# Attention and Hyena gate on one core: inverse transform of two batches on 193 columns and their mirror, with a new instruction sequence

## The chip, the cores and the metric

The kernel runs on one core of a Trainium2 chip. A core has a matrix engine, TensorE (PE in the profile, its weight loads apart as PEld), and three engines for element work: VectorE (DVE), ScalarE (ACT) and GpSimd (POOL). SyncE (SP) only issues DMAs. Each engine works off its own queue of instructions in order and waits on semaphores for the others. Operands lie in SBUF, a memory of 128 partitions; TensorE writes its results to PSUM, of which the kernel uses four slots of two banks. The metric is the device time of one execution in microseconds (us); less is better.

## The reference

Inputs are q, k, v with 4 batches, 8 heads, 768 positions and 64 numbers per head, and the matrices of the gate. Heads are either "retrieval" (full causal attention) or "streaming" (4 sink positions and a window of 64).

```python
scores = np.where(mask, scale * q @ k.transpose(0, 1, 3, 2), -1e9)     # per head
a = np.exp(scores - scores.max(-1)); a = a / (a.sum(-1) + 1e-09)
x = (a @ v).transpose(0, 2, 1, 3).reshape(B, S, H * D)                 # B=4, S=768, H*D=512
...
proj = x @ w_proj
x1, x2, x3 = proj[..., :D], proj[..., D:2*D], proj[..., 2*D:]          # D = 512 here
X2 = np.fft.rfft(x2, n=S, axis=1)
H = np.fft.rfft(filter_fft, n=S, axis=0)[None, :, :]
x2_conv = np.fft.irfft(X2 * H, n=S, axis=1)
y = x1 * x2_conv * x3
return (y @ w_out).astype(np.float32)
```

## The kernel before

**Two halves.** Attention is done in 16 units n = 0 to 15 of two heads each; units 4b to 4b+3 belong to batch b. The gate follows batch by batch, so that the gate of batch b runs while the attention of batch b+1 does. After unit 15 only the gate of batches 2 and 3 is left.

**An order written out by hand.** The whole fast path is one straight-line program. A string named FAST lists its steps; a word such as `oe3.1/s` or `c3.0.0@2` names a step, after "/" the engine that does it (v VectorE, s ScalarE, p GpSimd) and after "@" the PSUM slot that it takes. Steps without "/" have a fixed engine. A loop at the end of the function calls the steps in the order of the string, so the string sets the order of every engine's queue, and semaphores only what data and buffers ask for. Of SBUF the buffers are fixed too: a step that writes one waits for its last readers.

**Attention steps.** `lq`, `lk`, `lv` load (L908, L927, on the SP queue), `cq`, `ck` and from unit 8 on `cqk` cast q and k to bf16, with the source in one of three rotating buffers, two of which are named qk_ahead. `T` transposes the result: for units 0 to 7 on TensorE (L952), from unit 8 on as a DMA transposition on the SP queue (L962). `sc` are the scores (L990), `ex` the exponential (L1007), `mk` masks, `at` the product with v (L1050; v carries a column of ones, f_v_aug and its copy f_v_x), `rec` and `nm` the division (L1056, L1067). `fd`, `fe`, `fA`, `fS`, `fb`, `fr` add and subtract mirrored positions of a unit's output (f_fo, f_uv, f_br), which shortens the forward transform; `W` does that transform on TensorE (L1103 to L1111) and `We` evicts it to f_xh. `tn` brings the attention output into transposed form, for later units as a DMA transposition (L1132).

**Gate steps of batch b.** `X` (L1154) multiplies f_xh by w_proj, which gives the spectrum of x2 in three tiles t of 128 frequencies, real and imaginary part beside each other; `Xe` evicts them to bf16. `sw` swaps the halves of tile 2 by two DMAs (L1179, f_Xw). `pa`, `pb`, `pc` multiply by the filter's spectrum HAB and add: P, the product of spectra (all through the helper line L544). `x1` and `x3` are the other two projections (L1189), `xs` the eviction of x1. `c` (L1227) is the inverse transform of a block cb of 128 channels: r = 0 gives the part of the result that is even about the middle, r = 1 the odd part, each over 384 positions, from three matmuls with 384 columns each (cosine and sine tables Gi as the moving operand):

```python
for m, (t, u, tile_no) in enumerate(INVERSE[r]):
    nc.tensor.matmul(ps[:, r, 0:HS], lhsT=P(b)[:, t, u, ch], rhs=Gi()[:, tile_no],
                     start=(m == 0), stop=(m == 2))
```

Here HS = 384 and S = 768. `ce` copies the even part to SBUF (L541, f_evs, which lies in the buffer angle), `cv` (L1238) adds and subtracts the odd part, still in PSUM, and writes the 768 positions of the convolution in bf16 to f_conv, which lies in the buffer turns. There are two such buffers, for even and odd cb. `g` (L1208, L1212, L1214) multiplies x1 or the convolution by x3, `y` (L544) the convolution by what is left, into f_gy; `gh` (L1219) is the last half row of block 3 of batch 3. `o` (L1262; L1257 in halves for the row tile i = 5 of batch 3) multiplies by w_out, `oe` evicts to f_o and `st` stores.

**The end.** `rest` issues eight blank matmuls (L586). Steps `gd0` to `gd4` (L655 to L674) check that the row sums are sane: `gd0`, `gd1`, `gd2` reduce on VectorE, `gd3` is a one-column matmul, `gd4` writes a flag named `other`. `late` (L579) is a small cast that reads the last evictions. Then all engines read `other` (L1314) and skip a general path if it is 0.

## Time and profile before

| what | us |
|---|---|
| median of three runs (lowest, highest) | 183.8 (183.39, 184.66) |
| span of the profiled execution (the profile gives no other time of it) | 182.1 |
| TensorE busy in it | 172.8 |
| VectorE busy in it | 149.8 |
| ScalarE busy in it | 145.3 |
| GpSimd busy in it | 77.5 |

A page of the profile groups the instructions of one execution by line, engine and shape. "f_P<-f_X,f_HAB 128x1024 bf16" means that P was written from X and HAB, 1024 elements in each of 128 partitions. "x4 | 8.9, 2215" is the count, the busy time in us and the mean duration of one in ns; what follows is the idle time of the engine just before, with what ended it. A timeline row has the start, the duration and the same words; idle time stands in brackets at its end. In the chain of waits each row is a stretch of the path that ended last. L544 and L541 are lines of helpers that many steps share, so their rows are told apart by the names of the operands. Busy times of instructions that overlap on one engine are counted once, so a row "x2" may be shorter than twice one.

### The profile page before, as it was taken

The numbers are of one execution on the slowest core, as the hardware profiler recorded it, in microseconds if no ns is written. First come the engines' busy times: TensorE is split into PE (matmuls) and PEld (weight loads), VectorE is DVE, ScalarE is ACT, GpSimd is POOL, SyncE is SP. The second block draws the span as 40 slices with busy tenths as digits, with TensorE's granted clock in tenths as the row PEclk, the third lists the DMA queues.
The fourth block names the chain that finished last, engine by engine and source line by source line (L and its number), as shares of the span: only waits on it lengthen the run. The fifth ranks groups of instructions, "written<-read, shape, count | busy, mean of one in ns | idle before, by whom it ended". The sixth has DMA issues, their size and how long they took to land.

```text
span 182.1 us, 4374 instructions
## 1 busy us (share of the span) xinstructions
PE 172.8 (95%) x1684; PEld 103.6 (57%) x1700; DVE 149.8 (82%) x298; ACT 145.3 (80%) x196; POOL 77.5 (43%) x94
## 2 busy tenths in 40 slices
...
GB/s 159 356 203 287 294 257 200 204 290 230 232 224 166 184 228 198 116 214 142 265 217 200 150 231 166 123 208 243 228 153 112 184 0 0 58 2 119 127 277 184
DMA packets 78396, 33.83 MB, mean 186 GB/s; under 512 B 67618, under 2 KB 74786, under 8 KB 78370
## 3 DMA queue, kind: packets, MB, share of 16 engines
...
q8 instruction: 14, 0.23, 0.6%
...
q14 instruction: 12, 0.10, 0.2%
...
## 4 chain that ended last, share of the span: by engine, by line
PE 82%; DVE 8%; ACT 4%; DMA 3%; issue 1%
PE f_x_ps L1189 23%; PE f_X_ps L1154 12%; PE f_out_ps L1262 10%; PE f_c_ps L1227 9%; PE f_sc L990 8%; PE f_att L1050 7%; DMA f_qkT<-f_qk_bf 3%; PE f_qkT_ps L952 2%; PE f_sc L1001 2%; PE warm L454 2%; PE f_xt_ps L1123 2%; ACT f_pT L1007 1%; DVE f_HAB L691 1%; PE f_W_ps L1103 1%; PE f_W_ps L1105 1%
## 5 line engine op out<-in xcount | busy, mean ns | idle before, releaser
L1007 ACT ACTIVATE f_pT<-f_sc 128x1024 bf16<-128x1024 f32 (+3 forms) x68 | 58.5, 914 | 3.6 <-PE f_sc L990 2.0
L1189 PE MATMUL f_x_ps<-f_xT,f_wproj 128*128 128x384 bf16 x256 | 46.9, 326 | 0.0
L1189 PEld LDWEIGHTS <-f_wproj 128*128 128x128 bf16 x256 | 23.9, 98 | 17.4 <-issue 1.6
L990 PE MATMUL f_sc<-f_qkT 64*128 64x128 bf16 (+3 forms) x328 | 20.9, 242 | 2.4 <-DMA f_qkT<-f_qk_bf 1.4
L1154 PE MATMUL f_X_ps<-f_wproj,f_xh 128*128 128x512 bf16 x90 | 22.1, 379 | 0.6 <-issue 0.2
L544 POOL TENSOR_TENSOR f_fo<-f_attn 128x384 bf16<-128x384 bf16 x15 | 14.6, 990 | 18.4 <-DVE f_attn L1067 17.3
L1262 PE MATMUL f_out_ps<-f_wout,f_gy 128*128 128x512 bf16 x86 | 22.0, 379 | 0.3
L990 PEld LDWEIGHTS <-f_qkT 64*128 64x128 bf16 x328 | 11.4, 94 | 13.0 <-issue 7.9
L1238 DVE TENSOR_TENSOR turns<-angle,f_c_ps 128x384 bf16<-128x384 f32 x32 | 16.3, 550 | 2.6 <-ACT angle L541 1.3
L1227 PE MATMUL f_c_ps<-f_Gi,f_P 128*128 128x384 bf16 x96 | 18.2, 326 | 0.1
L1050 PEld LDWEIGHTS <-f_pT 128*128 128x128 bf16 x472 | 16.2, 97 | 2.4 <-issue 0.4
L1050 PE MATMUL f_att<-f_v_aug,f_pT 128*128 128x65 bf16 x392 | 17.0, 193 | 0.0
L541 ACT COPY f_o<-f_out_ps 128x1024 f32<-128x1024 f32 (+2 forms) x15 | 12.1, 818 | 6.2 <-PE f_out_ps L1262 5.1
L541 ACT CAST f_X<-f_X_ps 128x1024 bf16<-128x1024 f32 x12 | 12.1, 1016 | 4.9 <-PE f_X_ps L1154 4.9
L1067 DVE TENSOR_TENSOR f_attn<-f_att,f_recs 128x768 bf16<-128x768 f32 x16 | 15.1, 951 | 0.6
L544 POOL TENSOR_TENSOR f_P<-f_X,f_HAB 128x1024 bf16<-128x1024 bf16 x4 | 8.9, 2215 | 14.5 <-ACT f_X L541 14.5
L544 POOL TENSOR_TENSOR f_gy<-turns,f_gy 128x768 bf16<-128x768 bf16 x5 | 8.5, 1710 | 14.6 <-DVE turns L1238 14.6
L1154 PEld LDWEIGHTS <-f_xh 128*128 128x128 bf16 x96 | 8.9, 97 | 10.2 <-issue 0.5
L1262 PEld LDWEIGHTS <-f_gy 128*128 128x128 bf16 x92 | 8.5, 98 | 8.8 <-POOL f_uv L544 0.4
L541 ACT COPY angle<-f_c_ps 128x384 f32<-128x384 f32 x15 | 7.2, 478 | 7.7 <-PE f_c_ps L1227 5.4
L1227 PEld LDWEIGHTS <-f_P 128*128 128x128 bf16 x96 | 9.1, 98 | 6.0 <-issue 0.2
L537 POOL CAST f_qk_bf<-qk_ahead 128x768 bf16<-128x768 f32 (+1 forms) x9 | 8.0, 900 | 8.7 <-DMA qk_ahead<-in_k_dram 3.4
...
## 6 DMA issues: line engine op xcount, KB each, us to landing
...
```

Source lines behind the costliest of these rows:

```text
L537: nc.gpsimd.tensor_copy(out=out, in_=in_)
L541: nc.scalar.copy(out=out, in_=in_)
L544: (nc.gpsimd if now["engine"] == "p" else nc.vector).tensor_tensor(out, a, b, op)
L990: nc.tensor.matmul(sc[:, bank, col:col + 128 * cnt], lhsT=keys, rhs=qkT(n)[rows, 0, 128 * i:128 * (i + cnt)], start=(col == 0 or not biase ...
L1007: nc.scalar.activation(out=pT(n)[:, c, :, 0:w], in_=held[f"sc.{n}.{c}"][:, :, 0:w], func=AF.Exp, scale=SCALE)
L1050: nc.tensor.matmul(att[:, hh, 65 * i:65 * i + 65], lhsT=pT(n)[:, c, bank, col:col + 128], rhs=values, start=(z == 0), stop=(z == len(here) ...
L1067: nc.vector.tensor_mul(attn(n).rearrange("p i hh d -> p hh i d"), rows[:, :, :, 0:64], recs()[:, n][:, :, :, None].to_broadcast([128, 2, N ...
L1154: nc.tensor.matmul(ps[:, u, :], lhsT=xh(b)[:, cc, chain, 128 * part:128 * part + 128], rhs=wproj()[:, cc, DM:2 * DM], start=(cc == 0), sto ...
L1189: nc.tensor.matmul(ps[:, s, 0:HS], lhsT=wproj()[:, cc, part * DM + cb * 128:part * DM + (cb + 1) * 128], rhs=xT(b)[:, cc, s * HS:s * HS + HS],
L1227: nc.tensor.matmul(ps[:, r, 0:HS], lhsT=P(b)[:, t, u, ch], rhs=Gi()[:, tile_no], start=(m == 0), stop=(m == 2))
L1238: fn(conv[:, half * HS:half * HS + HS], held[f"evs.{b}.{cb}"], held[f"c_ps.{b}.{cb}"][:, 1, 0:HS])
L1262: nc.tensor.matmul(ps[:, i % 2, :], lhsT=gy(b)[:, cb, i * 128:(i + 1) * 128], rhs=wout()[:, cb, :], start=(cb == 0), stop=(cb == NC - 1))
```

## The change

**Fewer columns.** The even and the odd part are each made of two waves, one of which is symmetric and the other antisymmetric about position 192. For batches 2 and 3 (MIRROR) the inverse computes each wave at 193 positions alone, and the rest by mirroring. Per channel block and r there is one matmul of 386 columns (the tile that both waves share, against a new table Gb that holds it for both halves) and two of 193 columns, where there were three of 384. `ce` now copies 386 columns, `cv` has 386 columns and writes fp32 to `parts`, which lies with the copied even part in a qk_ahead buffer that attention no longer needs. Two new steps `cw` on VectorE for each block add and subtract the two halves and write the convolution in bf16, the second of them with the positions reversed. There are 16 of them.

**Smaller parts.** The new steps Gz, Gb0, Gb1, Gn fill the table Gb (one memset on GpSimd, two copies on ScalarE, a copy and a memset of one partition on VectorE). H0.0 and H1.0 write HAB once, 512 wide, where they wrote it twice, and `pa` for t = 0 and 1 reads it by broadcast.

**A new sequence.** FAST is replaced as a whole: 32 instructions go from GpSimd to VectorE, 28 from VectorE to GpSimd, 21 from ScalarE to VectorE, 23 the other way, 10 from ScalarE to GpSimd and 4 back. Among the moves are the casts cqk9, cqk10 and cqk13, from ScalarE to GpSimd. Steps gd1 to gd4 stand at the very end.

```diff
+MIRROR = (2, 3)
...
-cv3.3.0 x33.3.0 y3.2/v st2.5 st2.3 gd3@3 o3.0.0@2 o3.4.0@1 y3.3/v g3.3 gh o3.0.1 gd4 oe3.0/s o3.4.1 o3.1.0@0 o3.1.1
...
+cw3.3.1/v x33.3.1 y3.2/v o3.4.0@2 st2.5 o3.0.0@3 oe2.3/s o3.1.0@0 cw3.3.0/v y3.3/v g3.3 gh o3.4.1 oe3.4/s o3.0.1
...
+    Gb = C("Gb", [128, 2, 2, 194], BF16)
...
+    wave = lambda part, rows, tiles: Gi()[rows, tiles].rearrange("p t m f -> p t (m f)")[:, :, 0:193]
...
+            ev(Gb()[rows, :, half, 0:193], wave(half, rows, slice(2, 6, 3)))
...
+        nc.vector.tensor_copy(out=Gb()[64:65, 1, 0, 0:193], in_=wave(0, slice(64, 65), slice(5, 6))[:, 0])
+        nc.vector.memset(Gb()[64:65, 1, 1], 0.0)
...
-        scaled(f"H{t}.0", lambda t=t: HAB()[:, t, 0:2, :],
-               lambda t=t: FP(t)[:, 0, None, :].to_broadcast([128, 2, DM]), 2.0 / S)
+        scaled(f"H{t}.0", lambda t=t: HAB()[:, t, 0, :], lambda t=t: FP(t)[:, 0], 2.0 / S)
...
-                two(P(b)[:, t], held[f"X.{b}.{t}"], HAB()[:, t, 0:2], ALU.mult)
+                real = HAB()[:, t, 0:2] if t == 2 else HAB()[:, t, 0, None].to_broadcast([128, 2, DM])
+                two(P(b)[:, t], held[f"X.{b}.{t}"], real, ALU.mult)
...
+                    if b in MIRROR:
+                        (t0, u0, a), (t1, u1, z), (t2, u2, shared_tile) = INVERSE[r]
+                        waves = lambda tile_no: Gi()[:, tile_no].rearrange("p m f -> p (m f)")[:, 0:193]
+                        both = ps[:, r, 0:386].rearrange("p (h n) -> p h n", h=2)
+                        nc.tensor.matmul(both, lhsT=P(b)[:, t2, u2, ch], rhs=Gb()[:, shared_tile // 3, :, 0:193],
+                                         start=True, stop=False, skip_group_check=True)
+                        nc.tensor.matmul(both[:, 0], lhsT=P(b)[:, t0, u0, ch], rhs=waves(a), start=False, stop=True,
+                                         skip_group_check=True)
+                        nc.tensor.matmul(both[:, 1], lhsT=P(b)[:, t1, u1, ch], rhs=waves(z), start=False, stop=True,
+                                         skip_group_check=True)
+                        return
...
+            if b in MIRROR:
+                space = first[cb % 2].rearrange("p a h t d -> p (a h t d)")
+                parts = space[:, 0:772].rearrange("p (z n) -> p z n", z=2)
+                even = space[:, 772:1158]
...
+                    ev(even[:, 0:386], held[f"c_ps.{b}.{cb}"][:, 0, 0:386])
...
+                        fn(parts[:, half, 0:386], even[:, 0:386], held[f"c_ps.{b}.{cb}"][:, 1, 0:386])
...
+                        if half == 0:
+                            two(conv[:, :, 0:192], parts[:, :, 0:192], parts[:, :, 193:385], ALU.add)
+                        else:
+                            two(conv[:, :, 192:384], parts[:, ::-1, 192:0:-1], parts[:, ::-1, 385:193:-1], ALU.subtract)
```

**What stands where: the cast of unit 12.** In the rows below the first word is the line (the helper L541 of before is L543 now), then the operation, and output and inputs with the program's numbers. This is ScalarE's queue before, between the last exponentials of unit 11 and the gate of batch 1; `f_qk_bf_12` is the cast, `f_X_1_0` an eviction Xe1.0, `angle` the step xs1.2, `f_v_x2` a copy of v:

```order
L1007 ACTIVATE f_pT_10_1590<-f_sc_10_2_1727 128x1024
L541 CAST f_X_1_0_1765<-f_X_ps_1_0_1712 128x1024
L1007 ACTIVATE f_pT_11_1703<-f_sc_11_2_1735 128x1024
L541 CAST angle_87<-f_x1_ps_1_2_1754 128x768
L541 COPY f_v_x2_270<-f_v_aug2_248 64x520
L541 CAST f_qk_bf_12_1848<-qk_ahead0_66 128x1536
L541 COPY f_xT_2_1645<-f_xt_ps_9_1784 128x768
```

And now:

```order
L1026 ACTIVATE f_pT_10_1576<-f_sc_10_2_1732 128x1024
L1026 ACTIVATE f_pT_11_1718<-f_sc_11_2_1739 128x1024
L543 CAST f_qk_bf_12_1772<-qk_ahead0_66 128x1536
L543 CAST f_X_1_0_1778<-f_X_ps_1_0_1727 128x1024
L543 CAST angle_87<-f_x1_ps_1_2_1783 128x768
L543 COPY f_v_x2_133<-f_v_aug2_249 64x520
L543 COPY f_o_0_2_1855<-f_out_ps_0_2_1749 128x1024
L543 COPY f_xT_2_1645<-f_xt_ps_9_1819 128x768
```

The cast has moved ahead of Xe1.0, xs1.2 and the copy of v.

The same place on the SP queue, which issues the loads and DMA transpositions, before (`f_Xw` are the swaps of batch 1, `f_qkT` the transposition of unit 12, `f_xT` one of tn):

```order
L908 DMA qk_ahead_66<-in_q_dram 128x6x64 x2
L1179 DMA f_Xw_1719<-f_X_2_1671 64x1024
L927 DMA f_v_f_13_1721<-in_v_dram 128x6x64 x2
L1179 DMA f_Xw_1719<-f_X_2_1671 64x1024
L908 DMA f_qk_f_14_1762<-in_q_dram 128x6x64 x2
L908 DMA qk_ahead_69<-in_q_dram 128x6x64 x2
L962 DMA_TRANSPOSE f_qkT_1885<-f_qk_bf_1848 128x12x128
L1132 DMA_TRANSPOSE f_xT_1645<-f_attn_1905 128x6x128
```

And now:

```order
L927 DMA qk_ahead_66<-in_k_dram 128x6x64 x2
L946 DMA f_v_f_13_1769<-in_v_dram 128x6x64 x2
L1357 DMA out_dram<-f_o_0_1431 128x2x512
L1199 DMA f_Xw_1794<-f_X_2_1704 64x1024
L927 DMA qk_ahead_69<-in_q_dram 128x6x64 x2
L1199 DMA f_Xw_1794<-f_X_2_1704 64x1024
L981 DMA_TRANSPOSE f_qkT_1891<-f_qk_bf_1772 128x12x128
L927 DMA f_qk_f_14_1896<-in_q_dram 128x6x64 x2
L1151 DMA_TRANSPOSE f_xT_1645<-f_attn_1914 128x6x128
```

The load of unit 14 (f_qk_f_14) has moved behind the transposition, the second swap from ahead of both loads to a place behind the one that is left, and a store stands ahead of the first swap.

**What stands where: the products of batch 3.** VectorE's queue before, from the last cv of batch 2 to the middle of the products (`f_m` is what pb writes, `f_P` what pa and pc write, `f_sane` the step gd0):

```order
L1238 TENSOR_TENSOR turns<-angle,f_c_ps_2_2547 128x384
L1095 SCALAR_TENSOR_TENSOR f_br_2616<-f_uv_2585,f_fo_2558 128x256
L1238 TENSOR_TENSOR turns<-angle,f_c_ps_2_2547 128x384
L535 CAST f_xh_2470<-f_W_ps_2639 128x768
L544 TENSOR_TENSOR turns<-turns,f_x1s_3_2321 128x768
L1208 TENSOR_TENSOR f_gy_2676<-angle,f_x_ps_0_2647 128x768
L1212 TENSOR_TENSOR f_gy_2036<-turns,f_x_ps_3_2590 128x768
L544 TENSOR_TENSOR f_P_2702<-f_X_1_2690,f_HAB 128x1024
L544 TENSOR_TENSOR f_m_3_2_2734<-f_Xw_2687,f_HAB 128x1024
L655 TENSOR_SCALAR f_sane<-f_recs 128x192
L544 TENSOR_TENSOR f_P_2702<-f_P_2702,f_m_3_2_2734 128x1024
L544 TENSOR_TENSOR f_P_2702<-f_X_0_2704,f_HAB 128x1024
```

And now (`turns<-qk_ahead` is cw, `qk_ahead<-qk_ahead,f_c_ps` is cv):

```order
L546 TENSOR_TENSOR turns<-qk_ahead_69 128x2x192 x2
L1273 TENSOR_TENSOR qk_ahead_66<-qk_ahead_66,f_c_ps_2_2598 128x386
L1228 TENSOR_TENSOR f_gy_2665<-angle,f_x_ps_0_2655 128x768
L1273 TENSOR_TENSOR qk_ahead_66<-qk_ahead_66,f_c_ps_2_2598 128x386
L1232 TENSOR_TENSOR f_gy_2074<-turns,f_x_ps_3_2612 128x768
L546 TENSOR_TENSOR turns<-qk_ahead_66 128x2x192
L546 TENSOR_TENSOR f_P_2697<-f_X_2_2680,f_HAB 128x1024
L546 TENSOR_TENSOR turns<-qk_ahead_66 128x2x192
L546 TENSOR_TENSOR f_m_3_1_2726<-f_X_1_2695,f_HAB 128x1024
L546 TENSOR_TENSOR f_P_2697<-f_X_1_2695,f_HAB 128x1024
L546 TENSOR_TENSOR f_m_3_2_2744<-f_Xw_2689,f_HAB 128x1024
L546 TENSOR_TENSOR f_P_2697<-f_P_2697,f_m_3_1_2726 128x1024
```

The cw of batch 2 now stand among cv and the first product, and more of the products are on this engine. GpSimd's queue at that place before:

```order
L544 TENSOR_TENSOR f_gy_2036<-turns,f_gy_2036 128x768
L544 TENSOR_TENSOR f_P_2702<-f_X_2_2668,f_HAB 128x1024
L544 TENSOR_TENSOR f_m_3_1_2728<-f_X_1_2690,f_HAB 128x1024
L544 TENSOR_TENSOR f_P_2702<-f_P_2702,f_m_3_0_2742 128x1024
L544 TENSOR_TENSOR f_gy_2676<-turns,f_gy_2676 128x768 x2
```

And now:

```order
L546 TENSOR_TENSOR f_uv_2580<-f_fo_2517 128x2x128
L546 TENSOR_TENSOR f_uv_2580<-f_fo_2517 128x256
L546 TENSOR_TENSOR f_br_2596<-f_fo_2517,f_uv_2580 128x256
L546 TENSOR_TENSOR turns<-turns,f_x1s_3_2339 128x768
L546 TENSOR_TENSOR f_gy_2074<-turns,f_gy_2074 128x768 x2
L546 TENSOR_TENSOR f_gy_2665<-turns,f_gy_2665 128x768
```

Before these were y2.2, three products of batch 3, then y3.0 and y3.1. Now, behind the folds of unit 14, they are y2.3, y2.0, y2.2 and y3.1: the products and y3.0 have gone to VectorE, y2.3 and y2.0 have come from it.

**What stands where: the last blocks.** VectorE's queue before, from the inverse of batch 3 to its end (L665 is gd2, L674 gd4):

```order
L1238 TENSOR_TENSOR turns<-angle,f_c_ps_0_2758 128x384 x2
L665 TENSOR_REDUCE f_right<-f_sane 128x1
L1238 TENSOR_TENSOR turns<-angle,f_c_ps_1_2767 128x384 x2
L1238 TENSOR_TENSOR turns<-angle,f_c_ps_2_2783 128x384 x2
L1238 TENSOR_TENSOR turns<-angle,f_c_ps_3_2798 128x384 x2
L544 TENSOR_TENSOR f_gy_2676<-turns,f_gy_2676 128x768
L544 TENSOR_TENSOR turns<-turns,f_x1s_3_2755 128x768
L1214 TENSOR_TENSOR f_gy_2676<-turns,f_x_ps_3_2832 128x384
L1219 TENSOR_TENSOR f_gy_2676<-turns,f_x_ps_3_2832 128x384
L674 TENSOR_SCALAR other<-f_rows_right,differ 1x1
```

And now:

```order
L1273 TENSOR_TENSOR qk_ahead_69<-qk_ahead_69,f_c_ps_1_2765 128x386 x2
L1273 TENSOR_TENSOR qk_ahead_66<-qk_ahead_66,f_c_ps_0_2771 128x386 x2
L546 TENSOR_TENSOR turns<-qk_ahead_66 128x2x192 x2
L546 TENSOR_TENSOR turns<-qk_ahead_69 128x2x192 x2
L546 TENSOR_TENSOR f_gy_2665<-turns,f_gy_2665 128x768
L1273 TENSOR_TENSOR qk_ahead_66<-qk_ahead_66,f_c_ps_2_2803 128x386 x2
L1273 TENSOR_TENSOR qk_ahead_69<-qk_ahead_69,f_c_ps_3_2821 128x386 x2
L546 TENSOR_TENSOR turns<-qk_ahead_66 128x2x192 x2
L546 TENSOR_TENSOR turns<-qk_ahead_69 128x2x192
L546 TENSOR_TENSOR f_gy_2665<-turns,f_gy_2665 128x768
L546 TENSOR_TENSOR turns<-qk_ahead_69 128x2x192
L546 TENSOR_TENSOR turns<-turns,f_x1s_3_2719 128x768
```

Between the cv there now stand the eight cw of batch 3 and y3.0; the guard's steps are out of it.

144 lines of the change are left out of this document (82 added, 62 removed).

## The prediction

> **What bounds the kernel now.** I read the page's busy shares, then the busy times by stage, the chain of waits, and last the timelines of VectorE, GpSimd and the DMA queue at the two places where TensorE does not simply run on.
>
> ```profile
> PE 172.8 (95%) x1684; PEld 103.6 (57%) x1700; DVE 149.8 (82%) x298; ACT 145.3 (80%) x196; POOL 77.5 (43%) x94
> PE 82%; DVE 8%; ACT 4%; DMA 3%; issue 1%
> ```
>
> ```profile
> 0.00:42.00 42.00, 37.75 (x433) 22.55 (x439) 34.15 (x63) 37.40 (x54) 24.30 (x47) 1.00 1.03 250
> 42.00:98.00 56.00, 55.63 (x623) 34.88 (x626) 51.12 (x113) 53.25 (x69) 22.66 (x22) 1.00 1.04 200
> 98.00:138.50 40.50, 38.67 (x401) 23.84 (x404) 35.94 (x75) 37.51 (x51) 12.70 (x12) 1.00 0.98 191
> 138.50:173.40 34.90, 34.73 (x200) 19.38 (x201) 27.64 (x48) 14.12 (x20) 17.79 (x14) 1.00 0.27 71
> 173.40:182.10 8.70, 5.97 (x32) 2.93 (x30) 0.92 (x3) 2.99 (x6) 0.00 (x0) 1.00 0.61 224
> ```
>
> The columns of a stage are its length, then busy time of PE, PEld, DVE, ACT and POOL, the granted clock (1.00 throughout) and the DMA share. TensorE is the bound and works at the full clock: from 42 to 173.4 it stands still for hardly 2 us. In the last compute stage (138.5 to 173.4) it has no gap at all, while VectorE has 34.90 - 27.64 = 7.3 us free and ScalarE 20 us. So a TensorE instruction that is removed there is worth its time, as long as VectorE, which gets new work there, still keeps up. The one wait in the middle is the second place:
>
> ```profile
> 93.26 1.01 ACT L541 CAST f_X<-f_X_ps 128x1024 bf16<-128x1024 f32 x1 [0.16 <-PE f_X_ps L1154]
> 94.17 1.03 ACT L1007 ACTIVATE f_pT<-f_sc 128x1024 bf16<-128x1024 f32 x1
> 95.08 0.81 ACT L541 CAST angle<-f_x_ps 128x768 bf16<-128x768 f32 x1
> 95.91 0.62 ACT L541 COPY f_v_x<-f_v_aug 64x520 bf16<-64x520 bf16 x1
> 96.56 1.47 ACT L541 CAST f_qk_bf<-qk_ahead 128x1536 bf16<-128x1536 f32 x1
> ```
>
> ```profile
> 94.38 1.33 SPq L908 DMA_DIRECT2D f_qk_f<-in_q_dram  x2
> 95.75 2.27 SPq L908 DMA_DIRECT2D qk_ahead<-in_q_dram  x2
> 98.13 2.18 SPq L962 DMA_TRANSPOSE f_qkT<-f_qk_bf  x1
> ```
>
> ```profile
> 103.66 0.61 PE L990 MATMUL f_sc<-f_qkT 64*128 64x256 bf16 x6 [1.40 <-DMA f_qkT<-f_qk_bf]
> ```
>
> The cast of unit 12 ends at 98.03 on ScalarE, its transposition T12 is issued at 98.13, and the first scores of the unit start 5.5 us later, TensorE having waited 1.40 us for them. Before T12 the SP queue was busy without a break, so both the cast and the queue hold it.
>
> **The change, part by part.** *Inverse matmuls.* The rows are from the chain of waits:
>
> ```profile
> 46.83 1.34 PE f_qkT_ps L952 x24
> ...
> 139.83 3.41 PE f_c_ps L1227 x21
> ...
> 172.72 4.05 PE f_out_ps L1262 x18
> 176.77 0.87 PE f_out_ps L1257 x8
> ```
>
> One matmul of 384 columns takes 3.41 / 21 = 0.162 us, one of 128 columns 1.34 / 24 = 0.056. Between them 193 columns come to 0.056 + 65 x (0.162 - 0.056) / 256 = 0.083, and 386 to 0.163. Batches 2 and 3 had 2 x 4 x 2 x 3 = 48 matmuls, 7.8 us; they now have 16 x (0.163 + 2 x 0.083) = 5.3 us. That is **-2.5 us**. That weight loads limit the short matmuls is excluded by the 128-column row, which runs at 0.056 each with a load for each. Ends: -2.5 (all of it kept) and, if VectorE takes it back, the next term but one.
>
> *The cast of unit 12 and T12.* In the new sequence ScalarE does this cast ahead of the f_X eviction, the angle cast and the f_v_x copy (pitches of 0.9, 0.8 and 0.65 between the rows' starts): 2.4 us earlier. On the SP queue the pair of loads at 94.38 (1.33 us) moves behind T12, the one at 95.75 stays ahead, and the second swap of Xw goes behind that load instead of ahead of it, so T12 can be issued 1.33 us earlier, and of the two gains the smaller counts. The three ScalarE instructions now wait 1.5 us longer and the loads of unit 14 come 2.2 us later; the units' scores are 15 us on, so nothing is late with them. **-1.2 us** (0, if another wait stands behind; -1.4 at most).
>
> *VectorE after 138.5.* The groups of that stage (busy, mean ns of one, idle before), and one group of the opening:
>
> ```profile
> L1238 DVE TENSOR_TENSOR turns<-angle,f_c_ps 128x384 bf16<-128x384 f32 x16 | 8.2, 550 | 1.8 <-ACT angle L541 0.7 <-PE f_c_ps L1227 0.5 <-POOL f_gy L544 0.3
> ...
> L544 DVE TENSOR_TENSOR f_P<-f_P,f_m 128x1024 bf16<-128x1024 bf16 x2 | 1.4, 689 | 0.0
> L544 DVE TENSOR_TENSOR turns<-turns,f_x1s 128x768 bf16<-128x768 bf16 x2 | 1.1, 550 | 0.0
> L535 DVE CAST f_xh<-f_W_ps 128x768 bf16<-128x768 f32 x1 | 1.0, 958 | 1.5 <-PE f_W_ps L1107 1.5
> ...
> L544 DVE TENSOR_TENSOR f_br<-f_fo,f_uv 128x256 bf16<-128x256 bf16 x2 | 0.6, 284 | 0.0
> L660 DVE SCALAR_TENSOR_TENSOR f_sane<-f_recs,f_sane 128x192 bf16<-128x192 f32 x1 | 0.4, 352 | 0.0
> ...
> L665 DVE TENSOR_REDUCE f_right<-f_sane 128x1 bf16<-128x192 bf16 x1 | 0.3, 349 | 0.0
> ```
>
> ```profile
> L728 DVE SCALAR_TENSOR_TENSOR f_G<-f_base,f_turned 128x256 bf16<-128x256 f32 x4 | 1.6, 418 | 0.0
> ```
>
> No instruction of the trace is a cw (384 elements, both inputs fp32 in SBUF, one of each pair read backwards). From below stands L728 (two fp32 inputs, 256 elements, 0.42), from above L1238 (384 elements, 0.55 alone, 8.2 / 16 = 0.51 in a row). I take 0.47, since the element count is L1238's and pairs overlap: 16 x 0.47 = 7.5. Added besides: three products from GpSimd at 0.6 net of overlap, 1.8, and two of f_uv's kind, priced by the f_br row, 0.55. Out go one turns (0.5), one f_br (0.3), the f_xh cast that goes to ScalarE (0.9), and the two guard instructions L660 and L665 that go to the end (0.65). Net 7.5. The cv grow by 2 of 384 columns and the ce likewise: nothing. Room is 7.3 us idle; then what GpSimd now costs VectorE:
>
> ```profile
> 157.20 2.35 DVE L544 TENSOR_TENSOR f_m<-f_Xw,f_HAB 128x1024 bf16<-128x1024 bf16 x1 [0.18 <-DMA f_Xw<-f_X]
> ...
> 160.86 0.68 DVE L544 TENSOR_TENSOR f_m<-f_X,f_HAB 128x1024 bf16<-128x1024 bf16 x1
> ...
> 167.23 1.02 DVE L1238 TENSOR_TENSOR turns<-angle,f_c_ps 128x384 bf16<-128x384 f32 x2
> ```
>
> ```profile
> 148.85 1.63 POOL L544 TENSOR_TENSOR f_gy<-turns,f_gy 128x768 bf16<-128x768 bf16 x1 [2.90 <-DVE turns L1238]
> ...
> 156.43 2.57 POOL L544 TENSOR_TENSOR f_m<-f_X,f_HAB 128x1024 bf16<-128x1024 bf16 x1
> ...
> 166.92 3.24 POOL L544 TENSOR_TENSOR f_gy<-turns,f_gy 128x768 bf16<-128x768 bf16 x2 [2.78 <-DVE turns L1238]
> ```
>
> The product of 0.68 took 2.35 beside a GpSimd multiplication: 1.67 lost. The pair of L1238, whose one input lies in PSUM, took its usual 1.02 beside GpSimd, and GpSimd its usual 1.62 each. So room is 7.3 + 1.7 = 9.0, less the 2.5 by which the stage is to be shorter: 6.5, against 7.5 of new work. VectorE is 1.0 us short with not one idle moment. Some of it is made good since VectorE's last work need not end at the stage's end (TensorE has 4.05 us of output matmuls after it), some lost since cw2.2.0 waits for y2.0, the second of two y in a row on GpSimd (3.2 us), with the products of batch 3 queued behind it. I take **+1.2 us**. Ends: +0.1 (cw at 0.42, 16 x 0.05 less) and +2.5 (cw at 0.51, plus 1 us lost beside y2.2).
>
> The sequence sets y2.2 after all products, but on GpSimd's queue nothing holds it: it starts once cw2.2.1 is done, beside the next products. The Trainium skill has a rule for this, on the page "SBUF — State Buffer", section "SBUF: two separate sides": VectorE and GpSimd share a pair of ports under an exclusive lock for a whole instruction; a VectorE instruction with two SBUF inputs wants it, and whoever starts first blocks the other. The rows above agree with it. It speaks against this change, as every cw has both inputs in SBUF where the cv it is added to has one in PSUM. By that rule y2.2 costs its full 1.6 us, the term is 1.0 + 1.6 = 2.6 and the sum -0.8 (183.0 us); by the busy times alone the term is 1.0 and the sum -2.4 (181.4 us).
>
> *The end.* The guard's last three steps and the read of `other` now stand behind the last eviction:
>
> ```profile
> 176.81 1.25 ACT L541 COPY f_o<-f_out_ps 128x512 f32<-128x512 f32 x3 [0.23 <-PE f_out_ps L1262]
> ...
> 178.09 0.16 DVE L579 CAST f_sane<-f_o 1x2 bf16<-1x2 f32 x1 [3.17 <-ACT f_o L541]
> ```
>
> The span ends at 182.1, 4 us after this cast, when the last store has landed and the engines have branched. L660 and L665 are hidden (VectorE idled 3.17 us here). The one-column matmul now follows the blank ones, and then one small VectorE step: some 1.5 us after the cast, inside the 4. **+0.3 us** (0 to +0.9), since the half-size eviction oe3.6 is now last rather than last but one.
>
> *Opening and the rest.* Other casts, loads and DMA issues change places from 0 to 98. ScalarE sheds more work there than VectorE takes on, but the 4 us that TensorE idles in the first 42 hang on loads and on ScalarE in turn; whether the end of the opening moves forward or back, no row says. **0** (-1 to +1). Gz, Gb0, Gb1, Gn run in GpSimd's and ScalarE's gaps: 0. The smaller HAB write saves half of three evictions, off the path: 0.
>
> Sum -2.5 - 1.2 + 1.2 + 0.3 = -2.2. Against the span of 182.1 that is 179.9. The median of the runs shown is 183.8, 1.7 above that span; with the same 1.7 the time is **181.6 us**, -1.2%.
>
> **The rivals.** *Second: the cover holds.* Cw cost 0.42, y2.2 falls into a gap, the end costs nothing: -2.5 - 1.2 + 0.4 = -3.3, **180.5 us**. For it: the clean L1238 rows, and 20 us free on ScalarE. Against: 1.0 us short before any wait.
>
> *Third: VectorE becomes the bound of the last 35 us.* Tail +2.5 and end +0.9: -0.3, **183.5 us**. For it: the 1.67 us lost once already, and y2.2 free to start beside a product. It wins if TensorE waits for f_P before the first inverse of batch 3 for over 1 us. This is what the skill's rule above leads to.
>
> *Fourth, slower.* The casts of units 9, 10 and 13 go from ScalarE to GpSimd, whose queue holds them behind other work:
>
> ```profile
> 113.89 1.52 POOL L537 CAST f_qk_bf<-qk_ahead 128x1536 bf16<-128x1536 f32 x1 [3.14 <-ACT f_qk_bf L541]
> ```
>
> That cast is no slower there (1.52 against 1.47), and GpSimd is half empty. But if each comes late, each transposition makes TensorE wait 1.4 us as T12 did: 181.6 + 4.2 = **185.8 us**. Two late ones leave the time level (184.4); the sign turns from two on, and 1% is passed with the third.
>
> *Fifth: the saving is not there*, because fewer columns do not shorten a matmul: the 128-column row speaks against it, and 184.1 would result.
>
> **How the numbers follow.** A measurement of this kernel can tell about 1% from no change: under 181.96 is faster, over 185.64 slower. Forecast 0.44 (its own range 180.8 to 182.4; 0.30 of it faster), second 0.25, third 0.17, fourth 0.10, fifth 0.04. Faster 0.30 + 0.25 = 0.55; same 0.14 + 0.17 + 0.02 = 0.33; slower 0.10 + 0.02 = 0.12. The range runs from the second with an opening 0.9 better, 179.6, to the third with 0.7 worse, 184.2; it leaves out the fourth and the outer parts of others, 0.2 in all.
>
> **What would show it.** Inverse matmuls of 386 and 193 columns at 0.163 and 0.083 in the chain; no wait of f_sc for f_qkT near 102, and none at units 9, 10, 13; cw rows at 0.42 to 0.51; a product stretched to over 1.5 us beside y2.2 (third) or not (second); TensorE's gaps after 140, none now, at 1 us in sum. The forecast is wrong if these gaps exceed 2 us, or if the opening up to 98 shifts by more than 1 us.

## The result: slower, and the profile after

| | median us (lowest, highest) | runs |
|---|---|---|
| before | 184.57 (183.39, 187.1) | 5 |
| after | 200.72 (200.46, 203.77) | 5 |

The ratio is 1.092 (95% interval 1.086 to 1.099): 16 us slower, where 181.6 us was forecast and 184.2 was the upper end of the range. The profiled execution of after is its longest and slow one (203.77 us, span 202.18): its granted clock stood at 0.50 from 27.8 to 31.2 us; the other four have spans of 199.0 to 199.9.

The busy line of the page of after:

```profile
PE 178.6 (88%) x1700; PEld 105.2 (52%) x1700; DVE 169.5 (84%) x318; ACT 143.9 (71%) x193; POOL 82.4 (41%) x98
```

TensorE, 95% busy before, now stands still for 24 us; VectorE is busy 20 us longer. Where the time went is read from equal stages of the two traces. Each ends with the last matmul of a step: attention of unit 3, X of batch 0, c of batch 0, attention of unit 9, the first scores of unit 12 (here their start), attention of unit 15, the last output matmul, the end.

| stage | before | after | difference |
|---|---|---|---|
| to unit 3 | 32.8 | 37.8 | +5.0 |
| to X of batch 0 | 14.0 | 14.9 | +0.9 |
| to c of batch 0 | 23.5 | 29.1 | +5.6 |
| to unit 9 | 17.4 | 17.9 | +0.5 |
| to the scores of unit 12 | 16.0 | 14.7 | -1.3 |
| to unit 15 | 34.8 | 39.0 | +4.2 |
| to the last output matmul | 39.2 | 40.0 | +0.8 |
| to the end | 4.5 | 8.8 | +4.3 |

The busy times by stage, with the columns of the prediction's table; first three stages of before, those with the largest differences ahead of the end:

```profile
0.00:32.80 32.80, 28.81 (x380) 18.50 (x383) 25.06 (x51) 28.39 (x42) 19.06 (x39) 1.00 1.02 249
46.80:70.30 23.50, 23.45 (x283) 15.52 (x281) 22.94 (x46) 21.86 (x32) 10.68 (x9) 1.00 1.13 203
103.70:138.50 34.80, 34.37 (x349) 20.77 (x354) 30.58 (x65) 32.77 (x44) 10.19 (x10) 1.00 0.96 195
```

Then all of after (the stage to unit 15 in two pieces):

```profile
0.00:37.76 37.76, 32.99 (x383) 20.51 (x383) 26.08 (x57) 28.46 (x41) 19.96 (x42) 0.95 0.95 235
37.76:52.67 14.91, 14.05 (x90) 6.60 (x91) 13.14 (x23) 14.07 (x18) 6.27 (x9) 1.00 0.97 179
52.67:81.78 29.11, 24.60 (x284) 15.72 (x281) 25.17 (x45) 21.79 (x31) 12.12 (x11) 1.00 0.96 172
81.78:99.69 17.91, 17.71 (x209) 10.85 (x207) 16.58 (x29) 16.57 (x22) 9.50 (x10) 1.00 0.97 190
99.69:114.38 14.69, 14.69 (x164) 9.17 (x164) 14.09 (x30) 13.96 (x18) 9.27 (x8) 1.00 0.75 175
114.38:133.75 19.37, 17.81 (x161) 10.14 (x160) 18.83 (x33) 14.63 (x20) 7.94 (x8) 1.00 1.04 181
133.75:153.38 19.63, 17.19 (x195) 10.32 (x196) 19.46 (x38) 16.29 (x22) 4.99 (x4) 1.00 0.66 145
153.38:193.38 40.00, 37.74 (x228) 21.25 (x227) 35.81 (x66) 17.48 (x25) 12.35 (x10) 1.00 0.30 100
193.38:202.18 8.80, 1.82 (x9) 0.67 (x7) 0.36 (x2) 0.65 (x2) 0.00 (x0) 0.79 0.30 107
```

Little of the loss lies where the inverse was changed (40.0 against 39.2). The loss by unit 15 is 14.9 us, in stages in which nothing was changed but the sequence, the writes of HAB, what pa reads of it, and the filling of Gb. Some 2 us of it are this execution's: new_order_no_mirror (below), whose words are the same up to there and whose clock stayed at 1.00, takes 35.6 us to unit 3 and is 12.5 behind by unit 15. TensorE idles 4.5 us in the third, 4.0 in the two pieces to unit 15. The waits of TensorE in after, with sum, count and longest in us:

```profile
PE f_att L1069 <- DVE f_xh L537: 2.2, 1, 2.2
PE f_W_ps L1130 <- DVE f_fo L546: 2.1, 2, 1.4
...
PE f_sc L1009 <- ACT f_pT L1026: 1.4, 2, 1.2
PE f_out_ps L1317 <- DVE f_gy L1228: 1.1, 1, 1.1
PE f_qkT_ps L971 <- ACT f_qkT L543: 0.9, 1, 0.9
```

Before, the waits of TensorE besides those of its warm-up were one of 1.4 us, one of 0.7, one of 0.5 and small ones of 0.2 and 0.3. Now there are a dozen of 0.5 to 2.2 us on many causes, and none is large enough to be the cause by itself.

### The profile page after: what moved, and what is told of

It is laid out like the page before. It is cut to its first block, busy times and chain, and to the rows that moved or that the text cites. A ratio compares the mean times of both kernels' runs of the same rounds, so it can differ in the third digit from the quotient of the medians.

```text
span 202.2 us, 4423 instructions
## 1 busy us (share of the span) xinstructions
PE 178.6 (88%) x1700; PEld 105.2 (52%) x1700; DVE 169.5 (84%) x318; ACT 143.9 (71%) x193; POOL 82.4 (41%) x98
## 5 line engine op out<-in xcount | busy, mean ns | idle before, releaser
L1009 PE MATMUL f_sc<-f_qkT 64*128 64x128 bf16 (+2 forms) x328 | 22.0, 246 | 3.2 <-ACT f_pT L1026 1.4
L1317 PE MATMUL f_out_ps<-f_wout,f_gy 128*128 128x512 bf16 x92 | 23.2, 380 | 1.4 <-DVE f_gy L1228 1.1
L546 POOL TENSOR_TENSOR f_fo<-f_attn 128x384 bf16<-128x384 bf16 x14 | 13.0, 935 | 18.2 <-DVE f_attn L1086 10.8
L1069 PEld LDWEIGHTS <-f_pT 128*128 128x128 bf16 x472 | 17.4, 100 | 5.7 <-issue 3.6
L1069 PE MATMUL f_att<-f_v_aug,f_pT 128*128 128x65 bf16 x392 | 17.9, 197 | 2.5 <-DVE f_xh L537 2.2
L543 ACT COPY f_o<-f_out_ps 128x1024 f32<-128x1024 f32 (+2 forms) x15 | 12.0, 815 | 6.5 <-PE f_out_ps L1317 6.0
L543 ACT CAST f_X<-f_X_ps 128x1024 bf16<-128x1024 f32 x12 | 12.1, 1015 | 4.2 <-PE f_X_ps L1173 4.2
L546 POOL TENSOR_TENSOR f_br<-f_fo,f_uv 128x256 bf16<-128x256 bf16 x6 | 9.6, 1605 | 13.1 <-DVE f_uv L546 9.4
L1044 DVE TENSOR_TENSOR f_pT<-f_pT,mtab 128x1024 bf16<-128x1024 bf16 (+1 forms) x18 | 13.6, 774 | 0.0
L543 ACT CAST f_xh<-f_W_ps 128x768 bf16<-128x768 f32 x11 | 8.6, 793 | 5.8 <-PE f_W_ps L1126 3.9
L546 DVE TENSOR_TENSOR f_fo<-f_attn 128x384 bf16<-128x384 bf16 x18 | 11.9, 673 | 0.2
L543 ACT COPY f_qkT<-f_qkT_ps 128x768 bf16<-128x768 bf16 x10 | 7.8, 801 | 5.2 <-PE f_qkT_ps L971 4.2
L539 POOL CAST f_qk_bf<-qk_ahead 128x768 bf16<-128x768 f32 (+1 forms) x9 | 10.3, 1146 | 1.3 <-DMA qk_ahead<-in_k_dram 1.3
```

The source lines that it names most:

```text
L539: nc.gpsimd.tensor_copy(out=out, in_=in_)
L543: nc.scalar.copy(out=out, in_=in_)
L546: (nc.gpsimd if now["engine"] == "p" else nc.vector).tensor_tensor(out, a, b, op)
L1009: nc.tensor.matmul(sc[:, bank, col:col + 128 * cnt], lhsT=keys, rhs=qkT(n)[rows, 0, 128 * i:128 * (i + cnt)], start=(col == 0 or not biase ...
L1044: nc.vector.tensor_mul(some, some, tab.to_broadcast([128, 2, cols, 128]))
L1069: nc.tensor.matmul(att[:, hh, 65 * i:65 * i + 65], lhsT=pT(n)[:, c, bank, col:col + 128], rhs=values, start=(z == 0), stop=(z == len(here) ...
```

## The experiments

Ratios are to the kernel before, timed on the same chip; its medians in these runs were 184.06 to 184.98 us.

**The end of the program.** The guard's steps are put back to where they were, once, and moved to the end of the kernel before, alone, once. First *guard_back*, against after:

```diff
-c3.0.1 g3.1 ce3.1/s
+c3.0.1 g3.1 gd1 ce3.1/s
...
-cv3.0.1 cv3.0.0 o2.3.0@0
+cv3.0.1 cv3.0.0 gd2 o2.3.0@0
...
-gh o3.4.1 oe3.4/s
+gh gd3@1 o3.4.1 gd4 oe3.4/s
...
-st3.6/s gd1 gd2 late gd3@3 gd4
+st3.6/s late
```

> The changed kernel with the guard's steps gd1 to gd4 ahead of the last output matmuls again. Theory G (GpSimd's way out): in the changed kernel GpSimd reads `other` at 195.5 and is through its last drain only at 201.3, 3.5 us after SP's at 197.8; in the kernel before it had read it long before the end. With the guard early the end shrinks by 3 to 4 us: 197 us. Rival (the end is set by the last store and the other engines' branches): 200.5 us, no change.

The median was 201.95 us (198.72 to 202.71), without a ratio that could be taken: one execution at a granted clock of 1.0 took 198.7, three at 0.98 took 201.3 to 202.7. In its trace the last stage is 5.35 us, 3.4 less than in after, but the stage ahead of it takes 41.6 instead of 40.0, with the clock at 0.50 for 3.4 of them. So the end became shorter as expected; that the whole did rests on one execution, 198.7 against 200.5 for the fastest of after. Then *before_guard_late*, against before:

```diff
-g3.1 gd1 c3.0.1
+g3.1 c3.0.1
...
-ce3.1/s gd2 cv3.1.1
+ce3.1/s cv3.1.1
...
-st2.3 gd3@3 o3.0.0@2
+st2.3 o3.0.0@2
...
-gh o3.0.1 gd4 oe3.0/s
+gh o3.0.1 oe3.0/s
...
-rest@3 late
+rest@3 gd1 gd2 late gd3@3 gd4
```

> The kernel before with gd1 to gd4 at its end, as the change has them, and nothing else. Theory G (GpSimd, which reads `other` only then, has a way out that takes over 5 us): the end grows by 3 to 4 us, 187 to 188 us. Rival: hidden behind the last store, 184 us as before.

187.23 us, ratio 1.015 (1.006 to 1.023): some 2.7 us for four small steps, nearer to the theory than to the rival. Its last stage by busy times, 8.32 us against 4.5:

```profile
177.40:185.72 8.32, 1.89 (x9) 0.67 (x7) 0.36 (x2) 0.39 (x2) 0.00 (x0) 0.82 0.28 97
```

The compute in it is short. VectorE's last rows of after show the part that the prediction counted:

```profile
194.09 0.16 DVE L582 CAST f_sane<-f_o 1x2 bf16<-1x2 f32 x1 [2.09 <-ACT f_o L543]
195.24 0.20 DVE L677 TENSOR_SCALAR other<-f_rows_right,differ 1x1 int32<-1x1 f32 x1 [0.98 <-PE f_rows_right L672]
```

The flag is there 1.35 us after the start of the cast that reads the last evictions, as forecast (1.5). But 6.7 us follow. The trace also has records of the engines' sequencers, which read the flag, branch and drain. They give these times:

```text
us                  GpSimd's read   GpSimd's last branch   GpSimd's drain      SyncE's last drain   GpSimd's next record   span ends
before              173.50          175.26                 175.66 to 176.47    181.28               181.31                 182.12
before_guard_late   179.62          181.12                 181.52 to 182.33    181.94               184.90                 185.72
after               195.48          196.97                 200.52 to 201.33    197.79               201.38                 202.18
```

With the flag late, SyncE reads it together with GpSimd and is through 2.3 us later. GpSimd is past its branch after 1.5 us, but then has no record for 2.6 us (before_guard_late, behind its drain) or 3.5 us (after, ahead of it), and it is the last that the end of the span waits for. In before GpSimd had read the flag 8.6 us ahead of the end, and all this lay beside the output; there it is SyncE that comes last. The prediction's "4 us after this cast, when the last store has landed and the engines have branched" took the branch as cheap, and the branch was in truth hidden. What GpSimd does while it has no record isn't shown.

**Mirror and sequence apart.** *old_order_mirror* has the whole mirror, its tables and cw, in the sequence of before, with the guard early:

```diff
-cv2.0.0 x13.1.1@2
+cv2.0.0 cw2.0.0/v cw2.0.1/v x13.1.1@2
...
-T5.1@3 cq4/p sb3.0
+T5.1@3 cq4/p Gz/p sb3.0
...
-fA7/v oe0.1/s fr7
+fA7/v oe0.1/s Gb1/s fr7
```

> The sequence of before with nothing but the 193-column inverse added: cw on VectorE right behind cv, the four table steps at gaps. Theory S (the new sequence costs the time, the mirror does not): 2.5 us of TensorE saved, 0 to 2.5 given back on VectorE, 181 to 184 us. Rival M (16 cw make VectorE the bound of the last 35 us): 190 us or more.

191.68 us, ratio 1.046 (1.035 to 1.057). Up to unit 15 its stages are those of before within 0.5 us (16.0 is 14.5, see below), but the stage to the last output matmul is 45.7 us against 39.2: here VectorE is the bound of the tail, by TensorE's rows:

```profile
144.92 0.82 PE L1209 MATMUL f_x_ps<-f_xT,f_wproj 128*128 128x384 bf16 x4 [1.01 <-DVE qk_ahead L1273]
147.73 2.12 PE L1209 MATMUL f_x_ps<-f_xT,f_wproj 128*128 128x384 bf16 x12 [1.99 <-DVE qk_ahead L1273]
```

The cw of one block stand ahead of the cv of the next, whose PSUM slot TensorE wants. This is what rival M expected. So in the tail the new sequence does help the mirror: 40.0 against 45.7 us. *mirror_batch_2_only* has the mirror for batch 2 alone, in the sequence of before_cast_early (below), with one eviction moved from VectorE to ScalarE:

```diff
+MIRROR = (2,)
...
-cv2.0.0 x13.1.1@2
+cv2.0.0 cw2.0.0/v cw2.0.1/v x13.1.1@2
...
-x33.0.1@1 We15/v
+x33.0.1@1 We15/s
```

> The sequence of before with the cast early as above, the 193-column inverse for batch 2 alone, its eight cw behind their cv, and the eviction We15 on ScalarE. Theory V (VectorE's work ahead of the products of batch 3 is what the mirror costs): TensorE saves 1.25 us in c2, eight cw (3.8 us) less We15 (0.9) come ahead of the products, and X3 comes 1 to 2 us late: 183 to 185 us. Rival (VectorE's idle time covers them): 181.5 to 182.5 us.

192.22 us, ratio 1.041 (1.033 to 1.050), and 188.82 (1.016) without the mirror; neither theory nor rival allowed for so much. Between these two traces the last c of batch 2 comes about 1 us earlier and the X of batch 3 3.8 us later, which is then kept to the end. *new_order_no_mirror* has the sequence of after and the old inverse for all batches. Without cw it is cv that writes the convolution, so in this sequence block 3's overwrites block 1's, in the same buffer, before y2.1 has read it, and the output is another:

```diff
-MIRROR = (2, 3)
+MIRROR = ()
...
-fe14/v cw2.1.1/v We13/s cw2.1.0/v x32.2.1
+fe14/v We13/s x32.2.1
```

> The new sequence with three matmuls of 384 columns for every batch, without cw (the four table steps stay in, unused). Theory S: the loss stays, 198 to 203 us. Rival M: near 185 us.

202.45 us, ratio 1.099 (1.091 to 1.108). The sequence alone costs 18 us, the mirror alone 7, both together 16; the intervals of 1.099 and 1.092 (1.086 to 1.099) overlap, so what the mirror brings within the new sequence is small or nothing. In the tail TensorE idles 0.6 us here (with the clock at 0.50 for 3.4) and 2.3 in after. *new_order_old_engines* keeps the order of after and gives 118 steps the engine they had before:

```diff
-wrap0 sin1 ones0 mtab3 lk2 kz2/v ones1 ck0/s T0.1@3 sin2 size cos2 alt gr0/s cq0/v
+wrap0 sin1 ones0 mtab3 lk2 kz2/p ones1 ck0/v T0.1@3 sin2 size cos2 alt gr0/v cq0/p
```

> The changed kernel in the new order, but with every step on the engine that it had before (118 steps go back). Theory E (the steps that changed engines collide with GpSimd's: VectorE's instructions were stretched by 21 us against 9.5 before): more than half of the loss goes, 192 us or less. Theory O (the order alone, with its loads and casts, is at fault): 198 us or more.

218.11 us, ratio 1.185 (1.175 to 1.195). So the engine moves are not what costs; they fit the new order, which without them is worse still.

**Where in the sequence.** The words of before are kept up to a step, and those of after follow. *new_from_unit_15*, with the guard early, changes after at15.1:

```diff
-at15.1 rec14 rec15 pc2.2/p x32.1.0@0
+at15.1 pc2.2/p rec14 nm14/v rec15 fd14/p x32.1.1@3
```

> The sequence of before up to the attention of unit 15 (138 us), then the new sequence and the 193-column inverse, with the guard's steps ahead of the last output matmuls. In the changed kernel the stretch from unit 15 to the last output matmul took 40.0 us against 39.2 before: theory T (the new tail gives back the 2.5 us and 0.8 more): 183.5 to 186 us. Rival (the old order's folds and products don't fit the new tail, as with the old order and the mirror): 189 us or more.

188.09 us, ratio 1.016 (1.005 to 1.026): between the two expectations; even the part of the change that holds the mirror does not gain. *new_from_unit_8* changes after sc8.0:

```diff
-sc8.0@2 sc8.3@0 fd6/p g0.3
+sc8.0@2 chk Gz/p cqk9/p fe7/p g0.3
```

> The sequence of before up to the scores of unit 8 (about 73 us), the new sequence and the 193-column inverse from there on. In the changed kernel the attention of unit 7 ends 10.9 us later than before, and the last output matmul 15.7 us later. Theory F (the new order of the first 73 us is at fault by itself): that 10.9 us goes, 188 to 191 us. Rival L (what comes late in the first part only uncovers limits that the later part has anyway): 195 us or more.

201.21 us (ratio 1.092), which looked like the whole loss, but chk, 2.62 us on VectorE, had come to stand ahead of g0.3 by the seam. *new_from_unit_8_again* has chk and Gz where they were:

```diff
-sc8.0@2 chk Gz/p cqk9/p fe7/p
+sc8.0@2 cqk9/p fe7/p
...
-fb7/v cv9/s
+fb7/v chk cv9/s
```

> As new_from_unit_8, but chk (2.6 us on VectorE there, ahead of g0.3, with TensorE idle for 3.6) stands where the order before had it, and Gz in a gap. Theory F (the first 73 us of the new order cost 11 us by themselves): 189 to 192 us. Rival L: 195 us or more.

194.56 us, ratio 1.054 (1.048 to 1.060). This is above theory F's 192 and just below the rival's 195. By this difference about 6 of the 16 us come with the words ahead of unit 8, about 5 with those from there to unit 15 (its stages 19.7, 14.7 and 38.3 against 17.4, 16.0 and 34.8), and the rest lies in the tail and the end, as in after. The parts don't simply add up: after itself is 11.5 us behind when the c of batch 0 is done, and new_order_no_mirror 9.

**What it is in the new order.** First theory: VectorE and GpSimd stop each other more often. In after, VectorE's first fold of unit 0 took 1.88 us, where the shortest of its kind take 0.35, and TensorE waited:

```profile
24.25 1.88 DVE L546 TENSOR_TENSOR f_fo<-f_attn 128x384 bf16<-128x384 bf16 x1
```

```profile
26.19 0.66 PE L1130 MATMUL f_W_ps<-f_G,f_fo 128*128 128x384 bf16 x3 [1.42 <-DVE f_fo L546]
```

What VectorE's rows took beyond the shortest row of the same operands and shape sums to 20.5 us in after and 11.0 before (the expectations have 21 and 9.5). *fewer_collisions* moves eight casts and copies from GpSimd to ScalarE and six steps from GpSimd to VectorE, those beside which VectorE was stretched most:

```diff
-vx3/s vs3/p rec1 vs2/p nm1/v ex3.1 cq5/p fd1/p
+vx3/s vs3/s rec1 vs2/s nm1/v ex3.1 cq5/s fd1/p
...
-at3.1@3 cv5/p We1/s
+at3.1@3 cv5/v We1/s
```

> The changed kernel in its order, with 14 of GpSimd's steps that ran beside a stretched VectorE instruction moved away: eight casts and copies to ScalarE, six to VectorE (among them pb0.1, pc2.2 and y2.2). Theory C (VectorE's stretch of 21 us, 9.5 before, is what costs the time): stretch near 11 us and 190 to 194 us. Rival O (the order costs it, whatever the collisions): 198 us or more.

200.99 us, ratio 1.090 (1.081 to 1.099). The stretch fell from 20.5 to 9.0 us, less than before has, and the time did not move. The group of the folds shows that the cure took; in after, and then in fewer_collisions:

```profile
L546 DVE TENSOR_TENSOR f_fo<-f_attn 128x384 bf16<-128x384 bf16 x18 | 11.9, 673 | 0.2
```

```profile
L546 DVE TENSOR_TENSOR f_fo<-f_attn 128x384 bf16<-128x384 bf16 x18 | 7.9, 452 | 0.2
```

The theory falls. Second: VectorE simply has too much to do. *new_order_no_masks* leaves out the 39 multiplications by masks, 26 us of VectorE; *before_no_masks* does so in before.

```diff
-sc4.0@2 mk5.1 mk4.2 vs5/s Xe0.2/s
+sc4.0@2 vs5/s Xe0.2/s
```

> The changed kernel without the 39 mask multiplications on VectorE (so the attention is unmasked), 26 us of VectorE there. Theory V (VectorE has become the bound of the new order up to unit 15): 10 us or more go, 190 us or less. Rival O (waits that the order makes on all engines): less than 6 us, 195 us or more.

> The kernel before without the same 39 mask multiplications, 20 us of VectorE there. Where TensorE is the bound: 182 to 185 us, 2 us gone at most.

196.99 us, ratio 1.071 (1.063 to 1.080), 3.7 less than after; and 185.24, ratio 1.011, for before, which gains nothing by it. That falls on rival O's side. Between units 12 and 15, where VectorE was busy 19.46 of the last 19.63 us, 3.4 us are won (39.0 to 35.6). In the stage to c of batch 0 it is now free for 7.8 us, and the stage is only 2 us shorter (TensorE idle 3 us):

```profile
50.99:78.10 27.11, 24.06 (x283) 15.68 (x280) 19.34 (x36) 21.74 (x31) 12.51 (x11) 1.00 1.03 185
```

So load accounts for most of the 4.2 us ahead of unit 15, and for 2 of the 5.6 here. Third: the waits are made by the order, each by a step listed close behind what it needs. Besides the fold of unit 0 above, the trace of after shows these, on TensorE and on ScalarE:

```profile
54.56 0.50 PE L971 MATMUL f_qkT_ps<-identity,f_qk_bf 128*128 128x128 bf16 x6 [0.89 <-ACT f_qkT L543]
...
73.75 1.14 PE L1258 MATMUL f_c_ps<-f_Gi,f_P 128*128 128x384 bf16 x6 [0.78 <-ACT angle L543]
...
80.79 0.39 PE L1009 MATMUL f_sc<-f_qkT 64*128 64x512 bf16 x2 [1.16 <-ACT f_pT L1026]
```

```profile
79.33 0.48 ACT L543 COPY angle<-f_c_ps 128x384 f32<-128x384 f32 x1 [1.67 <-PE f_c_ps L1258]
```

T6.0 stands behind the eviction E6.1 of the other half of its own PSUM tile, c0.1.1 behind ce0.1 likewise, and ce0.3, itself held for 1.67 us, stands ahead of the exponential ex8.2 that the next scores wait for. *four_waits_undone* exchanges such neighbours:

```diff
-fe0/v sc2.3@2
+fe0/v cv2/v sc2.3@2
...
-T6.1@1 E6.1/s T6.0
+T6.1@1 T6.0 E6.1/s
...
-ce0.1/s c0.1.1 g0.1
+c0.1.1 ce0.1/s g0.1
...
-ce0.3/s ex8.2
+ex8.2 ce0.3/s
```

> The changed kernel with four steps written a few places earlier or later: T6.0 ahead of the eviction E6.1 of the other half of its tile, c0.1.1 ahead of ce0.1 (as c0.1.1 waited for the eviction of the half beside it), the exponential ex8.2 ahead of ce0.3 (which held it back in ScalarE's queue), fe0 ahead of cv2 on VectorE. Theory W (the loss is a sum of waits that the written order makes, each as long as TensorE's gap at that place): 0.9 + 0.8 + 1.2 + 0.7 us go, 3 to 3.6 in all: 197 us. Rival (each wait taken away is met again at the next late step): 199 us or more.

201.12 us, ratio 1.088 (1.081 to 1.094), which can't be told from after. The stage fell by 1.5 us (27.6): the waits of 0.89 and 1.16 are gone, but the transposition behind T6 now waits 1.01 instead of 0.66, a product of attention 0.52 that had not waited, and c0.1.1 still 0.59. From there on the trace is 1.8 us longer than that of after, and its clock stood at 0.50 for 3.4 of them. So no few neighbours are it. The last two runs exchange a whole stretch, all words from the last X of batch 0 to the first scores of unit 8. *new_order_in_stretch* puts the words of after, with their engines, into the kernel before:

```diff
-X0.0.0 Xe0.1/s te3/s mk5.2 T6.0@1 Xe0.0/s Hd1 cq7/p lw2.1 T7.0@2 T6.1 mk5.1 ck7/v T7.1 at5.1@3
+X0.0.0 chk Gk1 Hd0 cq7/p mk5.1 mk5.2 H2.3 H2.4 Xe0.1/s pa0.2/v Hd1 Xe0.0/s lq8 lw2.1 at5.0@0 at5.1 T6.1@1
```

> The kernel before, with the order and engines of the changed kernel in that stretch alone, without the 193-column inverse. Theory O: the stretch takes 27 us or more instead of 23.5, and the kernel 3 to 5 us longer, 187 to 190 us. Rival: 24.5 us or less, 185 us.

195.85 us, ratio 1.065 (1.058 to 1.073): 11 us lost without mirror, new table or late guard. In its trace the stretch takes 32.16 us, against 23.5 in before:

```profile
47.45:79.61 32.16, 25.95 (x285) 17.07 (x284) 26.89 (x50) 21.86 (x30) 11.55 (x11) 0.95 0.97 176
```

TensorE's rows with waits in it:

```profile
48.55 0.22 PE L1049 MATMUL f_att<-f_v_aug,f_pT 128*128 128x65 bf16 x2 [1.10 <-ACT f_X L540]
49.87 0.24 PE L1049 MATMUL f_att<-f_v_aug,f_pT 128*128 128x65 bf16 x2 [1.09 <-DVE f_pT L1024]
50.47 0.20 PE L1049 MATMUL f_att<-f_v_x,f_pT 128*128 128x65 bf16 x1 [0.37 <-DVE f_pT L1024]
...
52.47 0.80 PE L951 MATMUL f_qkT_ps<-identity,f_qk_bf 128*128 128x128 bf16 x6 [0.94 <-ACT f_qkT L540]
...
58.68 0.45 PE L989 MATMUL f_sc<-f_qkT 64*128 64x128 bf16 x8 [0.21 <-DVE f_qkT L534]
...
69.65 0.66 PE L1110 MATMUL f_W_ps<-f_G,f_fo 128*128 128x384 bf16 x3 [0.54 <-DVE f_fo L543]
...
71.58 1.14 PE L1226 MATMUL f_c_ps<-f_Gi,f_P 128*128 128x384 bf16 x6 [0.78 <-ACT angle L540]
...
78.62 0.39 PE L989 MATMUL f_sc<-f_qkT 64*128 64x512 bf16 x2 [1.16 <-ACT f_pT L1006]
```

The eight waits sum to 6.19 us, all of the 32.16 - 25.95 = 6.21 that TensorE idles. It is also busy 2.5 us longer than before (25.95 against 23.45); the clock behind the first gaps, 0.50 for 3.4 us (below), makes up to 1.7 (half of 3.4) of them. The rest isn't taken apart; in after the same stretch is busy 1.15 us longer at a clock of 1.00. The waits are of two kinds. The first three (2.56 us) belong to the seam and are not in after: X0.0 and at5 have the same slot here, and chk (2 us and more on VectorE) has come to stand ahead of mk5. The other five (3.63 us) are those of after again, the 0.9 of T6.0, the 0.78 of c0.1.1 and the 1.16 of ex8.2 among them, at the same steps. So the order of these words, with their engines, makes these waits by itself, whatever stands ahead of and behind them. The first three waits and the lower clock behind them are the seam's, and so a good part of the loss, which is over twice what was expected. The diff shows how they come about: before, T6.0, T7.0, T6.1 and T7.1 followed the last X at once, two slots in turn, and each eviction had the time of the next; after, both halves of T6 stand around the eviction of the one. Last the opposite, *old_order_in_stretch*, the words of before in the same place of after:

```diff
-X0.0.0 mk4.1 pa0.2/v Hd1 Xe0.0/s ck6/p lq8 lw2.1 at5.0@0 at5.1 T6.1@1 E6.1/s T6.0
+X0.0.0 Gk0 mk4.1 ck6/v te3/s T6.0@1 Xe0.0/s Hd1 lw2.1 T7.0@2 T6.1 ck7/v T7.1 at5.1@3
```

> The changed kernel, with the order and engines of before from the last X matmul of batch 0 to the scores of unit 8 (three or four steps differ at the ends). Theory O (the order makes the waits): the stretch takes 23.5 to 24.5 us instead of 27 to 29. What is left of it at the end is open: 196 us if the rest is as it was. Rival (what came late ahead of it causes them): 27 us or more for the stretch, 200 us.

201.71 us, ratio 1.093 (1.084 to 1.103). The stretch did come down, from 29.1 to 25.0 us, but the stage to unit 9 behind the seam grew by 1.7 and the time stayed where it was. Its mean clock was 0.973 to 0.984, and in its trace the clock stood at 0.50 twice for 3.4 us, from 25.3 and from 148.1, which costs up to 1.7 us each and is part of it; the rest isn't settled. The new words of this stretch bring their waits into the kernel before, and taking them out of after does not win the time back: how much each stretch is worth depends on what stands behind it.

**The cast of unit 12.** *before_cast_early* moves cqk12 ahead of Xe1.0 and T12 ahead of the load of unit 14, in before, as the change does:

```diff
-X1.0.0 g1.0 sw1.0 vs10/v vs11/v ex10.2 x11.2.0@1 pb1.1/v fe9/v lq14 Xe1.0/s
+X1.0.0 g1.0 vs10/v vs11/v ex10.2 x11.2.0@1 pb1.1/v fe9/v cqk12/s Xe1.0/s
...
-x31.1.0@3 T12 oe0.5/s
+x31.1.0@3 T12 lq14 oe0.5/s
```

> The kernel before with the cast of unit 12 ahead of Xe1.0 on ScalarE, and on the SP queue the load of unit 14 behind the transposition T12 and the second swap behind the load that is left. Theory B (as predicted): the wait of 1.40 us at 102 to 104 goes and 1.2 us with it, 0.6 to 0.7% faster. Rival: the next late step takes it, no change.

188.82 us, ratio 1.016 (1.008 to 1.023): slower by more than the noise, and not faster. ScalarE reached the cast before its input had landed, and the eviction behind it was late for TensorE:

```profile
96.60 1.47 ACT L540 CAST f_qk_bf<-qk_ahead 128x1536 bf16<-128x1536 f32 x1 [2.23 <-DMA qk_ahead<-in_q_dram]
```

```profile
99.03 0.49 PE L1122 MATMUL f_xt_ps<-identity,f_attn 128*128 128x128 bf16 x6 [2.59 <-ACT f_X L540]
```

*before_load_early* issues the load itself earlier, and *before_load_cast_early* does both:

```diff
-rec8 T10 lv10 nm8/v
+rec8 T10 lk12 lq12 lv10 nm8/v
```

> The kernel before with the two loads of unit 12 three places earlier on the SP queue (behind the transposition T10, ahead of lv10), nothing else. The cast stays in its place on ScalarE at 96.6. Theory (load and cast come at the same time, so the cast's place holds T12 as well): no change, 184.9 us. Rival (the load alone holds it): 1.2 us faster.

> The loads of unit 12 early as in before_load_early, and the cast and the SP queue's order as in before_cast_early. Theory: with its load there in time the cast no longer waits, T12 goes 1.3 us earlier and the wait of 1.40 us shrinks to 0.2: 1.2 us faster than before, 0.6%. Rival: lv10 and lv11, now 3 us later, hold units 10 and 11: no change or slower.

184.38 us, ratio 1.002 (0.998 to 1.007), and 186.51, ratio 1.015 (1.009 to 1.022). Neither gains. In the trace of before_load_early the wait of 1.40 us is gone, but TensorE waits as long for the transposition of unit 11, which is issued at 85.7 instead of 84.6, behind these loads:

```profile
90.15 0.56 PE L989 MATMUL f_sc<-f_qkT 64*128 64x128 bf16 x14 [1.51 <-DMA f_qkT<-f_qk_bf]
```

The 1.40 us in question aren't lost in every execution either: in before_guard_late and old_order_mirror, which have the words of before up to there (the second with three table steps between them), the stage took 14.5 us and TensorE did not wait for f_qkT at all. No kernel of this study beats the one before.

## Why the prediction was wrong, step by step

*Opening and the rest* is the step that failed. It was put at 0 (-1 to +1), on the ground that no row says whether the end of the opening moves forward or back. By unit 15 the profiled execution was 14.9 us behind, 16.2 without the stage of unit 12; without the clock's part, by new_order_no_mirror, it is 12.5. A missing row was taken for a small number. The reading that TensorE's idle time in the first 42 us hangs on loads and on ScalarE doesn't hold either: its largest waits there are 1.53 and 0.69 us for VectorE, then 0.46 and 0.30 for ScalarE, and none is for a load. The chain of waits should have warned: before, TensorE is 82% of it, that is, nearly every other engine's step is ready when TensorE comes to it. That is a property of the order, and a replaced order has to show that it keeps it. Afterwards the chain (of guard_back, which is after up to the last blocks) reads:

```profile
PE 46%; DVE 34%; ACT 11%; issue 5%; POOL 2%; DVEq 0%; POOLq 0%; ACTq 0%
```

TensorE is only 46% of it there, and VectorE 34%. The bounds of 1 us either way were therefore no bounds: with every stage full, little could be gained there, and much be lost. What the runs showed in its place: the new sequence alone loses 18 us (new_order_no_mirror), and a single stretch of its words, put into before, brings 3.63 us of its own waits with it. Why each wait of the new order arises is shown for the places above, not for all of them; that load decides between units 12 and 15 rests on one run, and what keeps the time up when the waits of one stretch are gone is open.

*Inverse matmuls, -2.5*: right in the pitch. Durations overlap, so the pitch is read from starts: in

```profile
182.68 0.32 PE L1250 MATMUL f_c_ps<-f_Gb,f_P 128*128 128x386 bf16 x1
182.85 0.24 PE L1252 MATMUL f_c_ps<-f_Gi,f_P 128*128 128x193 bf16 x1
182.93 0.24 PE L1254 MATMUL f_c_ps<-f_Gi,f_P 128*128 128x193 bf16 x1
183.01 0.33 PE L1250 MATMUL f_c_ps<-f_Gb,f_P 128*128 128x386 bf16 x1
```

the steps are 0.17, 0.08 and 0.08 (forecast 0.163 and 0.083). The fifth rival is out. From each start to the next start or the end, the inverse matmuls of batches 2 and 3 take 7.8 us before and 5.9 in after, 1.9 less and not 2.5: where a wait follows, the last short matmul counts with its whole 0.25.

*VectorE after 138.5, +1.2*: mis-sized. The stage to the last output matmul grew by 0.8, so against the 2.5 that TensorE was to save 3.3 came back, beyond the upper end of 2.5. (That term's lower end, +0.1, and the second rival's +0.4 for the same case don't agree.) TensorE now idles 2.3 us there, and four waits make 2.15 of them: three for VectorE (0.27, 1.05 and 0.26) and one for ScalarE (0.57). The third rival's mechanism took place: VectorE's product beside y2.2 on GpSimd, and cw2.2.0 held by y2.0,

```profile
169.22 0.56 DVE L546 TENSOR_TENSOR turns<-qk_ahead 128x384 bf16<-128x384 f32 x1 [0.47 <-POOL f_gy L546]
...
171.51 2.13 DVE L546 TENSOR_TENSOR f_P<-f_X,f_HAB 128x1024 bf16<-128x1024 bf16 x1
```

```profile
170.93 2.16 POOL L546 TENSOR_TENSOR f_gy<-turns,f_gy 128x768 bf16<-128x768 bf16 x1 [1.74 <-DVE turns L546]
```

The product took 1.45 us more than the 0.68 of a free one. The rule of the Trainium skill ("SBUF — State Buffer", section "SBUF: two separate sides") agrees with this row. The cw were 0.54 each (8.7 / 16) and 0.49 in a row, against 0.47 taken and 0.51 as the bound. But the rival's own sign failed: what TensorE then waited for over 1 us was not f_P but the output's f_gy:

```profile
179.21 2.53 PE L1317 MATMUL f_out_ps<-f_wout,f_gy 128*128 128x512 bf16 x11 [1.05 <-DVE f_gy L1228]
```

*The cast of unit 12 and T12, -1.2*: the number was right (-1.3) by luck, the reason not shown. The cast moved alone made before slower, since its load landed only then, and the wait is absent from some executions of the unchanged words.

*The end, +0.3*: a second step that failed. It was +4.3 in the trace and +2.7 in the timed runs of before_guard_late. The failed part is the cover: the branch and GpSimd's time behind it had lain beside the output.

The fourth rival, late casts on GpSimd, did not take place: no f_sc of after waits for a DMA transposition. It had the sign right and not the mechanism or the size: a slower outcome was given 0.12 on one named mishap, while the change replaced every word of the sequence.
